# Attention's scores, transposes and products in pairs of PSUM banks, with a re-planned order of the whole kernel

## The chip, the core and the metric

The kernel is one launch on one NeuronCore of a Trainium2 chip. The metric is device time in microseconds (us), from the median of several runs; lower is better. TensorE (PE in the rows) does matmuls, VectorE (DVE) and ScalarE (ACT) do the elementwise work and read PSUM, GpSimd (POOL) helps with elementwise work in SBUF, and SyncE (SP) issues every DMA.

## What is computed

Three stages follow one another: attention, a gated feed-forward (called MoE1 here), and a feed-forward with layer norm and a residual (MoE2). Everything is fp32 on the host side, weights of MoE1 and MoE2 arrive as 64-bit floats.

```python
# attention: q, k, v are [4, 8, 576, 64]
q_d, k_d, v_d = means over groups of 4 positions            # [.., 144, 64]
out_up    = repeat(softmax(q_d k_d^T / 8) v_d, 4)           # coarse part
out_local = softmax(q k^T / 8 where |i - j| < 4) v          # band of 7
x = (out_up + out_local) as [4, 576, 512]
# MoE1
xk, xr = mu * x + (1 - mu) * (x shifted by one position)    # mu_k, mu_r
x1 = sigmoid(xr w_r) * (relu(xk w_k)^2 w_v)                 # w_k, w_v: 512 x 1024, 1024 x 512
# MoE2
out = x1 + relu(layernorm(x1) * g w_ch1) w_ch2              # 512 x 2048, 2048 x 512
```

## The kernel before, in words

**Units of attention.** `attention(n, ...)` (line 453) handles one of 16 units: one batch entry and two heads, which lie on partitions 0 to 63 and 64 to 127. Per unit, in order:

- q and k are loaded and brought to a head-dimension-by-position layout (`qT`, `kT`), by DVE's transpose (line 542) or by TensorE (lines 553 to 562, tile `tq`) depending on the unit's mode `m{n}`. Sums over four positions (`qd`, `kd`) come from DVE or POOL (lines 582 to 585), or, in mode 3, from the same TensorE pass.
- the band: for each head one PSUM bank `sc`. A bf16 matmul with a mask (line 623) opens it, then 24 blocks of 24 queries by 32 keys are added (line 629; the profile counts two matmuls for a block). The contraction runs over 64 partitions, those of the head, and a block writes one of four groups of 32 output partitions. DVE takes the maximum (`mx`, line 640) and subtracts it (`e`, line 643), each once per head; ACT takes the exponential of both heads at once (line 646).
- the coarse part: `ds` (line 655), maximum on DVE (line 667), its scaling on DVE or ACT (lines 668 and 669), three exponentials on ACT (line 673).
- sums and reciprocals on DVE (lines 677 to 681), normalisation, and a transpose of the band into `pT`, copied to `PT`.
- the coarse weights are transposed on TensorE into `tp` in two halves `kt`, one bank each (line 707), each copied to `pdT` by ACT or DVE (lines 711 and 712).
- `up` (line 718) is the coarse product; ACT copies it to `ups`.
- `pv` (line 748) is the band's product in two halves, one bank each; DVE adds `ups` to each half and writes `xT` (line 762). The alternative path `join` is off in all units (`g0` to `g15` are 0).

**MoE1** runs over six chunks of 384 tokens. `prep` (line 785) mixes neighbouring positions on ACT, DVE and POOL. `moe_r` makes `psr`, `moe_k` makes `psk`, `accumulate` (line 847) adds into three banks `psv` (line 778 to 780: each fp32 product is three matmuls of high and low parts), and `moe_x` (line 858) multiplies on DVE and stores. **MoE2** makes `psh` and accumulates `pso` in six banks.

**Weights** come through `load_f32` (line 383): a 512 KB DMA into one of two buffers `w64`, two passes on ACT (lines 395 and 397), two on DVE (402 and 406), then a split into a high and a low part (`load_split`, line 410; low part at line 420). The order of the first loads is by priority, lowest first: `w_r` tile `kt` has `wr + wrs * kt`, the first half of `w_k` has `wka + wkas * kt`.

**PSUM** has 8 banks: three of `ps_v` (`pv0`, `pv1`, `pv2`), two of `ps_k` (`pk`), three of `ps_a` (`pa`). Attention of batch entries 1 to 3 takes its banks from the three of `pa`; batch entry 0 goes round `pa`, `pk`, `pv0` and `pv1` (`psa`, line 444), since MoE1 does not run yet.

**The order of work.** Nothing is issued where it is written. `Plan.add` collects operations with a cost, a priority and the buffers read and written. `Plan.order` (line 123) walks them as a list scheduler: each engine takes the ready operation that can start first, ties by priority, and buffers of one tag are handed out strictly in the order of the priorities of their first users (`turn`). All constants in `PRM` are priorities and choices for this planner. `Plan.issue` (line 228) emits the engines' queues in that order. Each engine then runs its own queue strictly in order. While MoE1's third accumulator is not yet in use, `issue` fills TensorE's planned pauses with dummy matmuls (`warm`, line 433) of 0.14 us planned each; they keep the engine busy and compute nothing. A first batch of 17 is planned at 4.5 us, and in batch entry 0 each `sc` and `ds` group begins with two more.

```python
free = {e: 0.0 for o in ops for e, *_ in o.ways}       # order(): all engines begin at 0
...
for _ in range(int((o.at - free) / fill_cost)):        # issue(): dummy matmuls in a pause
    fill()
```

Of the kernel before, what the change touches and what calls it, by code (L numbers as in the profile page):

```python
# [24 lines left out]
    thin=89.915, t0=-16.294, t1=-9.875, t2=6.158, t3=7.667, t4=48.796, t5=19.99, t6=6.382, t7=-23.592, t8=-0.47,  # L25
    t9=-5.238, t10=-2.702, t11=0.12, t12=5.747, t13=-8.176, t14=-15.681, t15=-4.758, m0=2, m1=1, m2=0, m3=3, m4=1,
    m5=0, m6=0, m7=2, m8=3, m9=0, m10=0, m11=0, m12=0, m13=0, m14=0, m15=0, g0=0, g1=0, g2=0, g3=0, g4=0, g5=0, g6=0,
    g7=0, g8=0, g9=0, g10=0, g11=0, g12=0, g13=0, g14=0, g15=0, h0=1, h1=1, h2=1, h3=1, h4=0, h5=0, h6=0, h7=0, h8=0,
    h9=0, h10=0, h11=0, h12=0, h13=0, h14=0, h15=0, dve=0.27, pool=0, ta=-14.632, u0=4.274, tl=26.492, tm=4222.228,
    ld=33.163, ldv=76.41, mu=-14.605, wr=-0.059, wrs=-31.134, wka=-33.615, wkas=7.94, wkb=12.502, wkbs=-165.286,  # L30
    wv=103.601, wvs=2.875, wld=0.932, d0=235.165, d1=108.349, d2=260.708, d3=463.399, d4=581.694, d5=82886.056,
    a1=13.725, a1s=43.62, a1l=52.7, a2=-1.632, a2s=26.831, a2l=56.61, a3=54.215, a3s=40.382, a3l=96.628, xr=-60.685,
    xrs=16.307, xk=22.171, xks=1.12, xrn=9, xrns=1.512, xkn=-4.695, xkns=17.37, w2a=10.707, w2as=1.55, w2=7.281,
    w2s=34.846, wc=10.079, wcs=106.739, m2q=8, sld=-6.173, x1=3, wcg=-39.001, p0l=11.872, p0=2.352, p0s=3.263,
    p0n=7.723, dp=684.729, ra0=-8.097, ra1=-1.757, ra2=3.642, ra3=4.616, ra4=-5.44, ra5=0, rb0=0.342, rb1=19.209,
    rb2=16.653, rb3=33.463, rb4=10.116, rb5=0, rx0=-2.918, rx1=-13.421, rx2=8.601, rx3=12.062, rx4=-2.926, rx5=5.409,
    ne=12, we=52.842, wes=25.704, wel=6.378,
# [23 lines left out]
class Plan:  # L61
# [8 lines left out]
    SYNC = {"PE": 0.21, "ACT": 0.16, "DVE": 0.14, "POOL": 0.2, "SP": 0.0, "CTL": 0.0}  # L70

# [51 lines left out]
    def order(self):  # L123
# [6 lines left out]
        free = {e: 0.0 for o in ops for e, *_ in o.ways}  # L130
# [10 lines left out]
        for k in sorted(range(nb), key=lambda k: first[k], reverse=True):  # L141
            turn[tag[k]].append(k)
# [85 lines left out]
    def issue(self, fill, fill_cost, until):  # L228

        end, seq = self.order()  # L230
        free = 0.0
        for i in seq:
            o = self.ops[i]
            for b in o.bufs:
                if b.t is None:
                    pool = b.pool if hasattr(b.pool, "tile") else b.pool()
                    b.t = pool.tile(b.shape, b.dtype, name=b.name, tag=b.tag, bufs=b.bufs)
            eng, cost, fn, _ = o.ways[o.way]
            if eng == "PE":
                if until.t is None:  # L240
                    for _ in range(int((o.at - free) / fill_cost)):
                        fill()
                free = o.at + cost
            fn()
        return end
# [20 lines left out]
def attn_moe_kernel(  # L266
# [164 lines left out]
    def warm_up(n=17):  # L431
# [10 lines left out]
    n_ps = [0]  # L442

    def psa(b, name):
        if b > 0:
            return Buf(ps_a, [P, 512], F32, "pa", 3, name)
        ring = [(ps_a, "pa", 3), (ps_k, "pk", 2), (ps_v, "pv0", 1), (ps_a, "pa", 3), (ps_k, "pk", 2),
                (ps_a, "pa", 3), (ps_v, "pv1", 1)]
        pool, tag, n = ring[n_ps[0] % len(ring)]
        n_ps[0] += 1  # L450
        return Buf(pool, [P, 512], F32, tag, n, name)

    def attention(n, T0, TL):
# [19 lines left out]
        join = PRM[f"g{n}"]  # L473

        def load(src, dst):
            if runs:
# [3 lines left out]
                ), w=[dst], lat=2.2)  # L480
                return
            if mode:
                for hp in range(2):
# [3 lines left out]
                    ), w=[(dst, hp)], lat=2.2)  # L487
                return
            for hp in range(2):
                for e in range(2):  # L490
# [4 lines left out]
                    ), w=[(dst, (hp, e))], lat=2.2)  # L495
# [121 lines left out]
        for h in range(2):  # L617
            sc = psa(b, "sc")

            def score(h=h, sc=sc):  # L620
                if first:
                    warm_up(2)
                nc.tensor.matmul(sc()[:, :G * 32], identb, maskb.rearrange("p g c -> p (g c)"),
                                 start=True, stop=False)
                for g in range(G):
                    for j in range(4):
                        i = 4 * g + j
                        m = min(32, S - QB * i)
                        nc.tensor.matmul(
                            sc()[32 * j:32 * j + m, 32 * g:32 * g + 32],  # L630
# [5 lines left out]
            add("PE", 0.8 + hold(2), pr(0.2), score, r=[qT, kT], w=[sc] + held, thin=True)  # L636
            mx = Buf(at, [P, G, 1], F32, "mx", 2)
            scv = lambda sc=sc: sc()[:, :G * 32].rearrange("p (g c) -> p g c", c=32)
            add("DVE", c_dve(192), pr(0.25),
                lambda mx=mx, scv=scv: nc.vector.tensor_reduce(mx()[:, :, 0], scv(), axis=AX.X, op=ALU.max),  # L640
                r=[sc], w=[mx])
            add("DVE", c_dve(192), pr(0.25),
                lambda mx=mx, scv=scv, h=h: nc.vector.tensor_tensor(
                    e()[:, h], scv(), mx().to_broadcast([P, G, 32]), op=ALU.subtract),
                r=[sc, mx], w=[(e, h)])
# [16 lines left out]
        add("PE", 1.0 + hold(2), pr(0.3), dscore, r=[qd, kd], w=[ds_] + held, thin=True)  # L662
# [5 lines left out]
        add([("DVE", 0.2, lambda: nc.vector.tensor_scalar_mul(mxd()[:, 0:3], mxd()[:, 0:3], -0.0078125), False),  # L668
             ("ACT", 0.15, lambda: nc.scalar.mul(mxd()[:, 0:3], mxd()[:, 0:3], -0.0078125), False)],
            0, pr(0.35), None, w=[mxd])  # L670
        for t in range(3):
# [7 lines left out]
        add("DVE", 0.18, pr(0.5), lambda: nc.vector.tensor_scalar_add(stat()[:, 0:15], stat()[:, 0:15], 1e-9),  # L679
            w=[stat])  # L680
# [20 lines left out]
        for kt in range(2):  # L701
            tp = psa(b, "tp")
            tpv = lambda tp=tp: tp()[:HS, :2 * SD].rearrange("p (h c) -> p h c", c=SD)

            def tpose(kt=kt, tpv=tpv):
                for t, q0 in enumerate((0, 64, SD - 64)):
                    nc.tensor.transpose(tpv()[:, :, q0:q0 + 64], pd()[:, t, HS * kt:HS * kt + HS], ident)

            add("PE", 0.47, pr(0.65), tpose, r=[pd], w=[tp], thin=True)

            add([("ACT", c_act(288, True), lambda kt=kt, tpv=tpv: nc.scalar.mul(pdT()[:, kt], tpv(), 0.25), False),
                 ("DVE", c_dve(288), lambda kt=kt, tpv=tpv: nc.vector.tensor_scalar_mul(
                     pdT()[:, kt], tpv(), 0.25), False)], 0, pr(0.7), None, r=[tp], w=[(pdT, kt)])
# [11 lines left out]
        if not join:  # L725
# [8 lines left out]
        for half in range(2):  # L734
            pv = psa(b, "pv")

            def pvmm(half=half, pv=pv):
                for kt in range(2 if join else 0):
                    for hp in range(2):
                        nc.tensor.matmul(  # L740
                            pv()[64 * hp:64 * hp + 64, :288],
                            vd()[:, 2 * hp + kt, :],
                            pdT()[:, kt, hp, 72 * half:72 * half + 72].unsqueeze(2).to_broadcast([HS, 72, 4]),
                            start=(kt == 0), stop=False,
                        )
                for g in range(3 * half, 3 * half + 3):
                    for hp in range(2):
                        nc.tensor.matmul(
                            pv()[64 * hp:64 * hp + 64, 96 * (g % 3):96 * (g % 3) + 96],
                            vw()[:, hp, g, :],  # L750
                            PT[:, hp, g, :],
                            start=not join, stop=not join or g % 3 == 2,
                        )

            if join:
                add("PE", 1.75, pr(0.85), pvmm, r=[vw, PTb, vd, pdT], w=[pv])
                add(psum_copy(288, lambda half=half: x()[:, u, 1 + 288 * half:1 + 288 * half + 288],
                              lambda pv=pv: pv()[:, :288]), 0, pr(0.9), None, r=[pv], w=[(x, (u, half))])
                continue
            add("PE", 0.67, pr(0.85), pvmm, r=[vw, PTb], w=[pv], thin=True)  # L760
            add("DVE", c_dve(288), pr(0.9),
                lambda half=half, pv=pv: nc.vector.tensor_tensor(
                    x()[:, u, 1 + 288 * half:1 + 288 * half + 288].rearrange("p (s r) -> p s r", r=4),
                    pv()[:, :288].rearrange("p (s r) -> p s r", r=4),
                    ups()[:, 72 * half:72 * half + 72].to_broadcast([P, 72, 4]),
                    op=ALU.add), r=[pv, ups], w=[(x, (u, half))])
# [80 lines left out]
    def accumulate(pv, f, last, ab, wt, prio):  # L847
        a, b_ = ab
        wh, wl = wt
        for t in range(TT):  # L850
            add("PE", MW, prio, lambda t=t: mm3(
                pv[t](), a()[:, t * P:t * P + P], b_()[:, t * P:t * P + P], wh(), wl(), f == 0, last),
                r=[a, b_, wh, wl], w=[pv[t]])
# [449 lines left out]
```

## Time and profile before

| | us |
|---|---|
| three runs | 770.59, 773.99, 775.18 (median 773.99) |
| the profiled execution | 771.95 |
| its span, first to last instruction | 770.2 |
| mean granted TensorE clock in it | 0.999 of full speed |

Times in the rows count from the span's start. Times of engines are busy times; a matmul's time in a row covers its way through the array, and matmuls overlap, so the step from one start to the next says what one costs.

### The profile page before, as it was taken

What the parts mean: (1) busy time and instruction counts of PE and PEld (TensorE: products, weight loads), DVE (VectorE), ACT (ScalarE), POOL (GpSimd) and SP (SyncE); (2) the same over time, 40 slices, a digit from 0 to 9 for tenths busy, and PEclk for the clock granted to TensorE, in tenths of its full rate; (3) what the DMA queues carried; (4) which work ended last, traced back from release to release, by engine and by line L of the source; (5) the groups of instructions that cost most, each with busy time, mean ns of one, the idle gap of its engine ahead of it and who ended that gap; (6) DMA issues with size and microseconds to landing.
All of it is one profiled execution on the core that took longest, in us unless ns stands there. A gap on an engine that the chain in (4) does not pass through costs nothing.

```text
span 770.2 us, 15665 instructions
## 1 busy us (share of the span) xinstructions
PE 753.6 (98%) x5816; PEld 650.2 (84%) x5816; DVE 524.6 (68%) x1083; ACT 398.2 (52%) x916; POOL 63.8 (8%) x113
## 2 busy tenths in 40 slices
PE   9999999999999999999999999999999999999997
PEld 6878787788788798888888888889889899889886
DVE  6899999998985959878889763486543364333233
ACT  6889997987884847868835431221421131111110
POOL 3101122112100000000110000020000020000000
PEclk9999999999999999999999999999999999999999
DMA  8997596867768895964689894379853347443322
GB/s 190 208 192 180 180 180 124 182 170 144 207 159 267 251 323 171 290 217 135 141 281 289 208 258 121 112 246 305 183 150 115 112 121 258 138 120 113 123 69 82
DMA packets 202854, 140.88 MB, mean 183 GB/s; under 512 B 127120, under 2 KB 160028, under 8 KB 202780
## 3 DMA queue, kind: packets, MB, share of 16 engines
q1 hardware_dynamic: 202780, 139.90, 66.6%
q8 instruction: 46, 0.75, 0.4%
q14 instruction: 28, 0.23, 0.1%
HBM read 107.88 MB, written 31.98 MB: 182 GB/s over the span
## 4 chain that ended last, share of the span: by engine, by line
PE 77%; DVE 10%; DMA 6%; ACT 4%; issue 2%; POOL 0%; SPq 0%; DVEq 0%; POOLq 0%; ACTq 0%
PE pso L779 8%; PE pso L778 8%; PE pso L780 8%; PE psh L778 7%; PE psh L779 7%; PE psh L780 7%; PE psk L778 4%; PE psv L778 4%; PE psk L780 3%; PE psk L779 3%; PE psv L779 3%; PE psv L780 3%; DMA w<-in_moe_w_ch_dram 3%; PE warm L433 2%; DVE tmu L802 1%
## 5 line engine op out<-in xcount | busy, mean ns | idle before, releaser
L778 PE MATMUL psh<-xn,sa 128*128 128x384 f32 x336 | 114.0, 339 | 2.4 <-DVE c L1114 1.2
L779 PE MATMUL psh<-xn,sa 128*128 128x384 f32 x336 | 113.6, 338 | 0.0
L780 PE MATMUL psh<-xn,sa 128*128 128x384 f32 x336 | 113.3, 337 | 0.0
L778 PEld LDWEIGHTS psh<-xn,sa 128*128 128x128 f32 x336 | 63.1, 188 | 11.0 <-DVE c L1114 2.1
L779 PEld LDWEIGHTS psh<-xn,sa 128*128 128x128 f32 x336 | 63.1, 188 | 6.1 <-DVE xn L1051 0.2
L780 PEld LDWEIGHTS psh<-xn,sa 128*128 128x128 f32 x336 | 63.1, 188 | 0.0
L379 ACT ACTIVATE c22h<-t 128x384 fp32r<-128x384 f32 x24 | 12.6, 525 | 83.7 <-DVE t L1106 78.6
L395 ACT ACTIVATE wf<-w 128x512 f32<-128x512 f32 x48 | 32.3, 673 | 17.4 <-DMA w<-in_moe_w_ch_dram 9.2
L402 DVE SCALAR_TENSOR_TENSOR wf<-wf,w 128x512 uint32<-128x512 uint32 x48 | 32.9, 687 | 11.1 <-ACT w L397 10.6
L379 ACT ACTIVATE kr<-psk 128x384 f32<-128x384 f32 x46 | 22.4, 488 | 25.2 <-PE psk L780 21.2
L379 ACT ACTIVATE c11h<-psh 128x384 fp32r<-128x384 f32 x23 | 11.3, 491 | 45.8 <-PE psh L780 45.7
L397 ACT ACTIVATE w<-w 128x512 uint32<-128x512 uint8 x52 | 35.0, 672 | 0.0
L843 DVE TENSOR_TENSOR kl<-kr,kh 128x384 fp32r<-128x384 f32 x43 | 23.8, 553 | 14.6 <-ACT kr L842 14.3
L1083 DVE SCALAR_TENSOR_TENSOR c11l<-psh,c11h 128x384 fp32r<-128x384 f32 x24 | 13.3, 554 | 29.1 <-ACT c11h L379 29.1
L802 DVE SCALAR_TENSOR_TENSOR tmu<-xT,oms,tmu 128x384 f32<-128x384 f32 (+1 forms) x64 | 31.7, 512 | 1.8 <-ACT tmu L796 1.8
L406 DVE SCALAR_TENSOR_TENSOR wf<-w,wf 128x512 uint32<-128x512 uint32 x48 | 32.7, 680 | 0.3
L1106 DVE TENSOR_TENSOR t<-psh,t 128x384 f32<-128x384 f32 x24 | 13.3, 554 | 28.5 <-PE psh L780 28.4
L1097 DVE TENSOR_TENSOR u<-psh,u 128x384 f32<-128x384 f32 x24 | 13.3, 555 | 27.2 <-PE psh L780 27.1
L379 ACT ACTIVATE c12h<-c 128x384 fp32r<-128x384 f32 x24 | 12.6, 525 | 37.0 <-DVE c L1110 36.9
L379 ACT ACTIVATE c21h<-c 128x384 fp32r<-128x384 f32 x24 | 12.6, 523 | 34.6 <-DVE c L1114 34.6
L796 ACT ACTIVATE tmu<-xT,vecs 128x384 f32<-128x384 f32 (+1 forms) x51 | 26.8, 539 | 6.9 <-DVE xrl L806 4.0
L1103 DVE TENSOR_TENSOR t<-psh,u 128x384 f32<-128x384 f32 x24 | 13.2, 552 | 20.2 <-PE psh L780 20.1
(527 smaller groups left out, 2164.5 us busy)
## 6 DMA issues: line engine op xcount, KB each, us to landing
sa<-s_dram SPq DMA_DIRECT2D x168, 256.0 KB, 2.7
w<-in_moe_w_ch_dram SPq DMA_DIRECT2D x32, 512.0 KB, 6.2
s_dram<-s SPq DMA_DIRECT2D x56, 256.0 KB, 4.0
vw<-in_v_dram SPq DMA_DIRECT2D x62, 96.0 KB, 4.0
x_dram<-r SPq DMA_DIRECT2D x18, 256.0 KB, 3.4
x1t<-x_dram SPq DMA_DIRECT2D x6, 768.0 KB
z_dram<-x1t SPq DMA_DIRECT2D x18, 256.0 KB, 2.7
zb<-z_dram SPq DMA_DIRECT2D x96, 48.0 KB, 2.8
```

The costliest lines, as they stand in the source:

```text
L379: return [("ACT", c_act(n, True), lambda: nc.scalar.activation(dst(), src(), AF.Relu), False), ("DVE", c_dve(n), lambda: nc.vector.tensor_ ...
L395: add("ACT", c_act(512), prio, lambda: nc.scalar.activation(f(), w64().bitcast(F32)[:, :, 1], AF.Abs, scale=2.0 ** -112), r=[w64], w=[f])
L397: add("ACT", c_act(512), prio, lambda: nc.scalar.activation(w64()[:, :, 0], w64().bitcast(U8).rearrange("p a (b c) -> p a b c", c=4)[:, :, ...
L402: lambda: nc.vector.scalar_tensor_tensor(fu(), fu(), 3, w64()[:, :, 0], op0=ALU.logical_shift_left, op1=ALU.bitwise_or),
L406: lambda: nc.vector.scalar_tensor_tensor(fu(), w64()[:, :, 1], 0x80000000, fu(), op0=ALU.bitwise_and, op1=ALU.bitwise_or),
L433: nc.tensor.matmul(warm()[:, :304], identb, isumb, start=True, stop=True)
L778: nc.tensor.matmul(ps, lh, rh, start=start, stop=False, skip_group_check=more)
L779: nc.tensor.matmul(ps, lh, rl, start=False, stop=False, skip_group_check=more)
L780: nc.tensor.matmul(ps, ll, rh, start=False, stop=stop, skip_group_check=more)
L796: add([("ACT", c_act(n, ap=1), lambda t=t, o=o, n=n, cur=cur, kt=kt: nc.scalar.mul(t()[:, o:o + n], cur(), mu[:, kt:kt + 1]), False), ("DV ...
L802: lambda t=t, o=o, n=n, prv=prv, kt=kt: nc.vector.scalar_tensor_tensor(t()[:, o:o + n], prv(), om[:, kt:kt + 1], t()[:, o:o + n], op0=ALU. ...
L843: add(either(C, lambda e: e.tensor_tensor(kl(), kr(), kh().bitcast(F32), op=ALU.subtract)), 0, prio, None, r=[kr, kh], w=[kl])
```

## The change

Attention's `sc`, `tp` and `pv` each take one tile of two neighbouring banks, and one instruction reads both. The scores of the two heads are issued alternately. PSUM is split anew: `ps_a` is one pair `pp` and one single bank `pa`; `ps_v` is one pair `pv` and the single bank `pv2`; MoE1's and MoE2's accumulators become a pair and a single bank. For batch entries 1 to 3 every `tq`, `ds` and `up` uses the single `pa`, and every `sc`, `tp` and `pv` the pair `pp`; batch entry 0 alternates between `pp` and `pv` for the pairs and goes round `pk`, `pk`, `pa` for the rest. Two tiny operations may now run on POOL. The path `join` is dropped. The planner lets each engine begin at a later time of its own, the first batch of dummies is 8, and all constants are new (among them `m1` from 1 to 3, `m4` from 1 to 4).

```diff
-    thin=89.915, ... m1=1, ... m4=1, ... wr=-0.059, wrs=-31.134, wka=-33.615, wkas=7.94, ...
+    thin=44.759, ... m1=3, ... m4=4, ... wr=8.408, wrs=-37.451, wka=39.719, wkas=-29.625, ...
...
+    START = {"PE": 1.78, "ACT": 2.0, "DVE": 2.6, "POOL": 6.6, "SP": 0.74, "CTL": 0.0}
...
-        free = {e: 0.0 for o in ops for e, *_ in o.ways}
+        free = {e: self.START[e] for o in ops for e, *_ in o.ways}
...
-    def warm_up(n=17):
+    def warm_up(n=8):
...
     def psa(b, name):
         if b > 0:
-            return Buf(ps_a, [P, 512], F32, "pa", 3, name)
-        ring = [(ps_a, "pa", 3), (ps_k, "pk", 2), (ps_v, "pv0", 1), (ps_a, "pa", 3), (ps_k, "pk", 2),
-                (ps_a, "pa", 3), (ps_v, "pv1", 1)]
+            return Buf(ps_a, [P, 512], F32, "pa", 1, name)
+        ring = [(ps_k, "pk", 2), (ps_k, "pk", 2), (ps_a, "pa", 1)]
...
+    def psp(b, name):
+        pool, tag = (ps_v, "pv") if b == 0 and n_ps[1] % 2 else (ps_a, "pp")
+        n_ps[1] += 1
+        return Buf(pool, [P, 2, 512], F32, tag, 1, name)
...
-        for h in range(2):
-            sc = psa(b, "sc")
+        sc = psp(b, "sc")
+        def scores():
+            if first:
+                warm_up(2)
+            for h in range(2):
+                nc.tensor.matmul(sc()[:, h, :G * 32], identb, mask, start=True, stop=False)
+            for g in range(G):
+                for j in range(4):
+                    for h in range(2):
+                        nc.tensor.matmul(sc()[32 * j:32 * j + m, h, 32 * g:32 * g + 32],
+                                         qT()[64 * h:64 * h + 64, ...], kT()[64 * h:64 * h + 64, ...],
+                                         start=False, stop=(g == G - 1))
+        add("PE", 1.25 + hold(2), pr(0.2), scores, r=[qT, kT], w=[sc] + held, thin=True)
+        add("DVE", c_dve(384), ...  tensor_reduce(mx()[:, :, :, 0], scv(), max)
+        add("DVE", c_dve(384), ...  tensor_tensor(e(), scv(), mx().to_broadcast([P, 2, G, 32]), subtract)
...
-        add([("DVE", 0.2, ... mxd scale ...), ("ACT", 0.15, ...)], ...)
+        add([("POOL", 0.42, ... mxd scale ...), ("ACT", 0.15, ...)], ...)
-        add("DVE", 0.18, ... stat + 1e-9 ...)
+        add([("DVE", 0.35, ... stat + 1e-9 ...), ("POOL", 0.42, ...)], ...)
...
-        for kt in range(2):
-            tp = psa(b, "tp")        # three transposes, one copy of 288
+        tp = psp(b, "tp")            # six transposes, one copy of 576
...
-        for half in range(2):
-            pv = psa(b, "pv")        # twelve matmuls, one add of 288
+        pv = psp(b, "pv")            # 24 matmuls, one add of 576
...
-        pvs[c] = [Buf(ps_v, [P, 512], F32, f"pv{t}", 1, f"psv{t}") for t in range(TT)]
+        pvs[c] = accs(ps_v, "pv", "pv2", "psv")          # a pair and a single bank
...
-                    pv = [Buf(... f"pv{n}" ... if n < TT else ... "pa", 3 ...) for n in range(2 * TT)]
+                    pv = accs(ps_v, "pv", "pv2", "pso") + accs(ps_a, "pp", "pa", "pso")
-    add("PE", 4.5, -20.0, warm_up, w=[warm])
+    add("PE", 1.55, -20.0, warm_up, w=[warm])
```

## Rows read from the trace of the kernel before

**Rows 1.** The stretches: busy us and instructions by engine, granted clock, DMA share, GB/s.

```profile
0.00:60.00 60.00, 55.79 (x973) 43.35 (x974) 49.16 (x114) 45.03 (x120) 9.57 (x38) 1.00 1.00 196
60.00:235.00 175.00, 171.79 (x2266) 140.57 (x2265) 159.94 (x351) 148.76 (x386) 30.45 (x55) 1.00 0.72 169
235.00:390.00 155.00, 151.62 (x734) 131.90 (x733) 124.64 (x248) 111.41 (x225) 8.85 (x9) 1.00 0.76 227
390.00:771.00 381.00, 374.35 (x1849) 334.37 (x1847) 190.82 (x372) 93.05 (x185) 14.94 (x12) 1.00 0.56 169
```

**Rows 2.** Groups by line on PE: count, busy us, mean ns, idle before them.

```profile
L433 PE MATMUL warm<-isum,identb 128*128 128x304 bf16 x135 | 22.8, 308 | 2.0 <-DVE identb L326 1.8 <-issue 0.2
...
L778 PE MATMUL psk<-xkh,wk00h 128*128 128x384 f32 x24 | 9.2, 381 | 3.2 <-ACT r L822 2.6 <-ACT kr L379 0.6
```

**Rows 3.** The chain that ended last, 45 to 59 us: start us, us, what.

```profile
45.61 6.70 DMA w<-in_moe_w_r_dram
...
52.90 0.26 ACT ups L371
...
55.44 0.37 DVE xT L762
...
57.01 0.84 DVE wr0l L420
```

**Rows 4.** The timeline of PE: the first product of MoE1.

```profile
57.31 0.49 PE L778 MATMUL psr<-wr0h,xrh 128*128 128x512 f32 x1
```

**Rows 5.** The timeline of PE, one unit's scores: start us, us, engine, line, operation.

```profile
105.87 0.26 PE L623 MATMUL sc<-maskb,identb 128*128 128x192 bf16 x1
106.05 0.61 PE L629 MATMUL sc<-kT,qT 64*32 64x32 f32 x48
106.60 0.26 PE L623 MATMUL sc<-maskb,identb 128*128 128x192 bf16 x1
...
107.33 0.46 PE L655 MATMUL ds<-kd,qd 64*64 64x144 f32 x4
```

**Rows 6.** The timeline of PE's weight loads, the same stretch.

```profile
106.05 0.50 PEld L629 LDWEIGHTS sc<-kT,qT 64*32 64x32 f32 x48
```

**Rows 7.** The tile sc: count, duration ns min/median/max, first and last start us.

```profile
L629 PEld LDWEIGHTS sc<-kT,qT x1536: 95/109/110, 10.8 to 219.8; 64*32 64x32 f32 x192
...
L623 PE MATMUL sc<-maskb,identb x32: 243/256/258, 10.6 to 219.2; 128*128 128x192 bf16 x32
```

**Rows 8.** Groups by line on DVE up to 410 us: count, busy us, mean ns.

```profile
L762 DVE TENSOR_TENSOR xT<-pv,ups 128x288 f32<-128x288 f32 x32 | 13.8, 443 | 1.0 <-PE pv L748 0.9
...
L640 DVE TENSOR_REDUCE mx<-sc 128x6 f32<-128x192 f32 x32 | 10.9, 346 | 1.0 <-PE sc L629 0.7
L643 DVE TENSOR_TENSOR e<-sc,mx 128x192 f32<-128x192 f32 x32 | 10.9, 343 | 0.2
...
L684 DVE TENSOR_TENSOR e<-e,stat 128x384 f32<-128x384 f32 x16 | 8.8, 547 | 0.0
L677 DVE TENSOR_REDUCE stat<-e 128x12 f32<-128x384 f32 x16 | 8.6, 537 | 0.2 <-ACT e L646 0.2
...
L585 DVE TENSOR_REDUCE qd<-qT 128x144 f32<-128x576 f32 x10 | 7.4, 740 | 0.0
...
L679 DVE TENSOR_SCALAR stat<-stat 128x15 f32<-128x15 f32 x16 | 4.0, 248 | 0.2 <-ACT pd L673 0.2
```

**Rows 9.** Groups by line on ACT, the same stretch.

```profile
L711 ACT ACTIVATE pdT<-tp 72x288 f32<-72x288 f32 x27 | 10.0, 400 | 1.0 <-PE tp L707 0.8
```

**Rows 10.** The timeline: first write and last read of scores, a later unit.

```profile
168.44 0.26 PE L623 MATMUL sc<-maskb,identb 128*128 128x192 bf16 x1
...
171.52 0.36 DVE L643 TENSOR_TENSOR e<-sc,mx 128x192 f32<-128x192 f32 x1
```

**Rows 11.** The timeline: first write and last read of scores, unit 2.

```profile
25.05 0.25 PE L623 MATMUL sc<-maskb,identb 128*128 128x192 bf16 x1
...
35.53 0.35 DVE L643 TENSOR_TENSOR e<-sc,mx 128x192 f32<-128x192 f32 x1
```

More of the change, by code (lines that the diff above doesn't have):

```diff
@@ L30 @@
[L30 to L34, printed above, removed]
@@ L140, in order @@
         turn = {t: [] for t in slots}
-        for k in sorted(range(nb), key=lambda k: first[k], reverse=True):
+        for k in sorted(range(nb), key=lambda k: (first[k], k), reverse=True):
             turn[tag[k]].append(k)
@@ L634, in score @@
                         )
[L636 to L645, printed above, removed]
+        add("PE", 1.25 + hold(2), pr(0.2), scores, r=[qT, kT], w=[sc] + held, thin=True)
+        mx = Buf(at, [P, 2, G, 1], F32, "mx", 1)
+        scv = lambda: sc()[:, :, :G * 32].rearrange("p h (g c) -> p h g c", c=32)
+        add("DVE", c_dve(384), pr(0.25),
+            lambda: nc.vector.tensor_reduce(mx()[:, :, :, 0], scv(), axis=AX.X, op=ALU.max), r=[sc], w=[mx])
+        add("DVE", c_dve(384), pr(0.25), lambda: nc.vector.tensor_tensor(
+            e(), scv(), mx().to_broadcast([P, 2, G, 32]), op=ALU.subtract), r=[sc, mx], w=[e])
         add("ACT", c_act(384), pr(0.35), lambda: nc.scalar.activation(e(), e(), AF.Exp, scale=0.125), w=[e])
@@ L678, in attention @@
                                             op=ALU.add), r=[e], w=[(stat, 0)])
-        add("DVE", 0.18, pr(0.5), lambda: nc.vector.tensor_scalar_add(stat()[:, 0:15], stat()[:, 0:15], 1e-9),
-            w=[stat])
+        more = lambda e: (lambda: e.tensor_scalar_add(stat()[:, 0:15], stat()[:, 0:15], 1e-9))
+        add([("DVE", 0.35, more(nc.vector), False), ("POOL", 0.42, more(nc.gpsimd), False)], 0, pr(0.5), None, w=[stat])
         add("DVE", 0.2, pr(0.5), lambda: nc.vector.reciprocal(stat()[:, 0:15], stat()[:, 0:15]), w=[stat])
@@ L723, in upper @@
                     )
-        if not join:
+        if True:
             up = psa(b, "up")
@@ L733, in attention @@
         x = xT[b]
-        for half in range(2):
-            pv = psa(b, "pv")
[L737 to L766, printed above, removed]
@@ new lines, in attention, with pvmm @@
+        pv = psp(b, "pv")
+        def pvmm():
+            for g in range(G):
+                for hp in range(2):
+                    nc.tensor.matmul(
+                        pv()[64 * hp:64 * hp + 64, g // 3, 96 * (g % 3):96 * (g % 3) + 96],
+                        vw()[:, hp, g, :], PT[:, hp, g, :], start=True, stop=True)
+        add("PE", 1.4, pr(0.85), pvmm, r=[vw, PTb], w=[pv], thin=True)
+        add("DVE", c_dve(576), pr(0.9),
+            lambda: nc.vector.tensor_tensor(
+                x()[:, u, 1:1 + S].rearrange("p (f s r) -> p f s r", f=2, r=4),
+                pv()[:, :, :288].rearrange("p f (s r) -> p f s r", r=4),
+                ups().rearrange("p (f s) r -> p f s r", f=2).to_broadcast([P, 2, 72, 4]),
+                op=ALU.add), r=[pv, ups], w=[(x, (u, 0)), (x, (u, 1))])
@@ L851, in accumulate, with accs @@
             add("PE", MW, prio, lambda t=t: mm3(
-                pv[t](), a()[:, t * P:t * P + P], b_()[:, t * P:t * P + P], wh(), wl(), f == 0, last),
-                r=[a, b_, wh, wl], w=[pv[t]])
+                pv[t][0](), a()[:, t * P:t * P + P], b_()[:, t * P:t * P + P], wh(), wl(), f == 0, last),
+                r=[a, b_, wh, wl], w=[pv[t][1]])
+    def accs(pool, pair, one, name):
+        b2, b1 = Buf(pool, [P, 2, 512], F32, pair, 1, name), Buf(pool, [P, 512], F32, one, 1, name)
+        return [(lambda: b2()[:, 0], (b2, 0)), (lambda: b2()[:, 1], (b2, 1)), (b1, b1)]
     x1d = Fixed(x1_dram)
```

81 lines of the change are left out of this document (40 added, 41 removed).

## The prediction

> **What bounds the kernel now.** I read the stretches first, then the groups of TensorE by line, then the chain of waits, and last the timelines of single units. The stretches [rows 1] show four stages. From 390 us on, MoE2 keeps PE busy for 374.35 of 381 us, with DVE at half and ACT at a quarter: this stage is matmuls alone, and the change only gives its accumulators other banks. From 235 to 390 us and from 60 to 235 us PE stands idle for no more than 3.4 and 3.2 us, so PE sets the pace there too; but DVE is busy for 159.9 of 175 us in the second of these, ACT for 148.8, and a late elementwise step shows directly as a PE pause (the first `psk` product waits 2.6 us in all on ACT's `r`, and takes 381 ns in the mean [rows 2]). The first 60 us are different: 22.8 us of PE's busy time are dummy matmuls [rows 2]. There PE waits for the start of MoE1, and the chain shows for what: a load of `w_r` that takes 6.7 us and lands at 52.3, ACT's copy of `ups` standing behind it, DVE's add to `xT`, and the low part of `w_r` at 57.0 [rows 3]. Only then begins the work that fills PE (the first `psr` at 57.3 [rows 4]). So a microsecond counts if it is PE work between 60 and 390 us, or if it lies on the chain of the start; a microsecond of PE work among the dummies is worth nothing. All through, the granted clock is full [rows 1].
>
> **Scores.** One head costs 0.73 us from mask to mask (105.87 to 106.60), the two 1.46 (to 107.33, when `ds` begins): 0.18 from a mask to the first score and 0.55 for 48 small matmuls, twice [rows 5]. After the change there are two masks in a row, one change of shape and 96 small matmuls whose row halves alternate. The second mask I put at 0.10, an estimate below the 0.18 that a mask takes together with the change of shape. If the heads' matmuls overlap fully, the 96 take 0.55 and the group 0.83; if they only queue, 1.10 and 1.38. So a unit saves 0.08 to 0.63 us. The nearest row is the issue of the weight loads: 48 of them span 0.50 us [rows 6], one takes 0.109 [rows 7], so one starts every (0.50 - 0.11) / 47 = 8.3 ns. At that rate 96 take 0.80 and a unit saves 0.38. I take 0.35, which is also the middle. Twelve units lie after the start: 12 x 0.35 = 4.2 us, with ends 1.0 and 7.6. The four units of batch entry 0 lie among the dummies: nothing.
>
> The Trainium skill ("TensorE: Matmul & The Clock Gate", Part 3: Packing small matmuls) says that a weight load overlaps matmuls in flight only where the row group differs, and that packed tiles start some 4 ns apart. In the kernel before all 48 scores of a group lie in one row group, and they still come 11 ns apart [rows 5], so the first half of the rule is too strict here; by the second half 96 scores would take 0.38 us, and a unit would save 1.46 - 0.66 = 0.80 us, 9.6 in all, an estimate by that page. The same page (Wait — 56ns, not 53.3ns?) gives a floor of about 25 ns between starts however small the matmul; by it neither form could be as fast as the 11 ns that the rows show, so it is set aside.
>
> **Elementwise work.** Two maxima of 346 ns become one of 384 columns; the sum over 384 columns takes 537 [rows 8]. Two subtractions of 343 become one, as the product over 384 in 547. Saved: 155 + 139 = 294 ns a unit. The two adds of 443 become one of 576 columns: at (537 - 346) / 192 = 1.0 ns a column 443 + 288 = 731, saved 155. Together 0.45 us of DVE a unit, 7.2 us over 16. The addition of 1e-9 (248 ns [rows 8]) may move to POOL, up to 4.0 us more. On ACT two copies of 400 ns [rows 9] become one of at least 400 and at most 800. In unit 1 the sums over four positions (740 ns each [rows 8], on DVE or POOL) give way to TensorE and four short copies.
>
> What reaches the end of it: after the start 12 x 0.45 = 5.4 us of DVE are freed where PE's own idle time is 3.2 + 3.4 us [rows 1]. It can return between nothing and 6.6 us; I take 2, because most of DVE's queue is not what PE waits for. A new order could also lose here: as much again, -4, is the lower end.
>
> **Transposes and products.** Their PE work is the same, in one group instead of two. Where two groups of `tp` stood apart, a change of shape goes, worth up to the 0.18 us of [rows 5]: 12 x 0.1 = 1.2 us, ends 0 and 2.2.
>
> **The start.** Four units free 4 x 0.45 = 1.8 us of DVE, unit 1 up to 1.5 more. The weights come in another order. By the old constants `w_r` tile 0 (-0.06) stands behind all four tiles of `w_k` (-33.6 to -9.8); by the new ones (8.4) only behind two (-49.2 and -19.5), so it is the sixth load instead of the eighth. That is the load on the chain [rows 3]. But unit 3 has its own tail there: `xT` at 55.4, only 1.6 us before the low part. If the load came early and the tail stayed, 1.6 us would be won; if ACT no longer stood waiting for it, up to 6. I take 3, with 0 as the lower end. `w_k` tiles 1 and 0 come behind instead; they are needed after MoE1's first gate products, which cover them. Fewer first dummies (8 instead of 17) cost nothing as long as the fill makes up for them and the granted clock stays full as in [rows 1]; no row shows a unit of attention at a lower clock, and what it would cost would fall among the dummies.
>
> **The accumulators** change banks only. A pair comes free when both its readers are done, but between two uses lie MoE1's gate and first `psk`, or MoE2's first `psh` products, several us long: nothing.
>
> **The sum:** 4.2 + 2 + 1.2 + 3 = 10.4 us, from the profiled execution's 771.95 (span 770.2 and 1.75 around it): 761.6. The median of the runs shown stands 2.0 above that execution; I add half of this for a median of new runs: 762.5.
>
> **Rivals.** *Little happens:* the heads' matmuls queue (1.0 us), the tail of unit 3 holds the start behind another weight load (1 us), and the waits stay: 771.95 - 2 + 1 = 771. For it speaks that PE, DVE and the DMA (share 1.00 in the first 60 us [rows 1]) are all full in the start; against it, that scores surely lose one change of shape.
>
> *The start comes much earlier:* with `w_r` early and ACT not standing behind it, MoE1 begins at 51 instead of 57 (6 us), scores overlap fully (7.6), changes of shape go (2.2) and waits fall by 4: 771.95 - 19.8 + 1 = 753. For it: the chain [rows 3] has a DMA and ACT's wait in it. Against: all ends at once.
>
> *The pair becomes the bound (slower):* three groups of each unit share one pair that is handed out strictly in the planner's order. A unit starts every (219.2 - 10.6) / 15 = 13.9 us (the last row of [rows 7] has the first and last mask). Scores hold their banks for 3.4 us where DVE comes quickly [rows 10], but for 10.8 us in unit 2 (25.05 to 35.88 [rows 11]). The mechanism decides from a mean hold of 13.9 / 3 = 4.6 us. Its price: in the start one hold of 10.8 instead of 3.4 in front of the next unit's groups, 7.4 us on the chain; afterwards each late unit delays a `prep`, and PE has no dummies any more; 12 units at 0.8 us are 9.6. With 4.2 + 1.2 saved as above: 771.95 + 7.4 + 9.6 - 5.4 + 1 = 784.5; at half the price it is 776. For it: three banks shrink to one pair and one bank. Against: the pair's readers are fewer and shorter, and attention is not on the chain between its batch entries.
>
> **How the numbers follow.** The forecast 0.50 (own range 756 to 769), little 0.22, much earlier 0.12, the pair as bound 0.16. A measurement of this kernel tells about 1% (7.7 us) from no change, so faster ends at 766.3. Of the forecast's 0.50 some 0.42 lie below that; with the early start 0.54. Slower by over 1% is above 781.7: the pair's case at over four fifths of its price, or with a lost order (-4) beside it, 0.13. The rest, 0.33, lies within 1%. The range leaves out the far half of the early start and the far part of the pair's case: 752 to 783.
>
> **What would show it.** Scores: one group of masks and 96 matmuls of 1.0 to 1.2 us; 0.83 would say full overlap, 1.38 none. DVE: one maximum and one subtraction of about 540 ns, an add of about 730, and DVE's total 7 to 11 us lower. The start: the first `psr` at about 54 instead of 57.3, and fewer than 20 us of dummies. MoE2: unchanged at some 380 us. The prediction is wrong if the first `psr` is later than 58, if PE has idle stretches before `sc`, `tp` or `pv` released by DVE's read of the pair, or if pauses between 60 and 390 us grow by more than 4 us.

## The result: slower by 1.2%, and the profile after

The changed kernel takes 779.24 us (median of 6 runs, 778.38 to 787.03) beside 771.27 us (770.19 to 775.18) for the kernel before on the same chip: ratio 1.0121, 95% interval 1.0092 to 1.0149. Its profiled execution is 778.71 us (span 776.9), 6.8 us above that of before.

The stretches after, which answer to [rows 1], with one more of 20 us:

```profile
0.00:60.00 60.00, 57.04 (x896) 45.16 (x897) 47.36 (x97) 41.51 (x111) 11.26 (x41) 1.00 0.92 185
60.00:235.00 175.00, 165.77 (x2336) 134.88 (x2335) 158.94 (x306) 147.99 (x373) 33.71 (x68) 0.99 0.76 177
235.00:390.00 155.00, 152.44 (x740) 133.18 (x739) 120.06 (x243) 111.10 (x223) 5.49 (x5) 1.00 0.72 214
...
80.00:100.00 20.00, 15.48 (x184) 11.64 (x187) 19.39 (x37) 17.10 (x42) 3.43 (x5) 0.91 0.62 161
```

TensorE's idle time between 60 and 235 us grew from 3.2 to 9.2 us, two thirds of the growth between 80 and 100 us (4.5 us idle; 0.6 before). There the granted clock fell too: to 0.5, the lower of its two levels, from 88.3 to 91.7 us. TensorE had stood still for 1.9 us (2.3 without a weight load) and was standing still again, for 1.0 us. I counted TensorE's instructions of both kernels at the step that each kind usually has in the kernel after. By that count, an estimate good to about 1 us, the two are level at 80 us; after is 4.3 us behind at 100, 5.2 at 250 and 4.2 at 760; the last 10 us add 1.9. So the loss has two places, and the pauses of both show in TensorE's waits and timeline.

TensorE's waits from 60 to 400 us in the kernel after (who, for whom: us in total, times, longest):

```profile
PE up L727 <- ACT pdT L720: 2.2, 3, 1.9
PE pv L748 <- ACT w L399: 1.6, 1, 1.6
PE psk L770 <- ACT kr L381: 1.3, 2, 0.8
PE tp L716 <- DVE xT L754: 1.3, 2, 1.1
PE tp L716 <- ACT pd L700: 1.0, 1, 1.0
...
PE psv L770 <- DVE r L858: 0.7, 1, 0.7
PE pv L748 <- ACT pdT L720: 0.7, 1, 0.7
```

The timeline of after in three places: one unit's scores, the pair handed from one unit to the next, and the last accumulation round:

```profile
83.47 0.81 PE L716 MATMUL tp<-isum,pd 128*72 128x128 f32 x6
...
86.15 0.64 ACT L720 ACTIVATE pdT<-tp 72x576 f32<-72x576 f32 x1
...
86.84 0.71 PE L727 MATMUL up<-pdT,vd 72*64 72x144 f32 x8 [1.85 <-ACT pdT L720]
...
91.60 1.24 PE L748 MATMUL pv<-PT,vw 128*64 128x96 f32 x24
95.58 0.76 DVE L754 TENSOR_TENSOR xT<-pv,ups 128x576 f32<-128x576 f32 x1
...
96.55 1.21 PE L748 MATMUL pv<-PT,vw 128*64 128x96 f32 x24 [1.62 <-ACT w L399]
...
110.73 0.34 PE L633 MATMUL sc<-maskb,identb 128*128 128x192 bf16 x2
...
111.00 1.01 PE L641 MATMUL sc<-kT,qT 64*32 64x32 f32 x96
...
111.94 0.95 PE L664 MATMUL ds<-kd,qd 64*64 64x144 f32 x12
...
764.55 0.39 PE L772 MATMUL pso<-w27h,c12l 128*128 128x512 f32 x1
764.98 0.69 DVE L1135 TENSOR_TENSOR res<-pso,res 128x512 f32<-128x512 f32 x1 [1.75 <-PE pso L772]
...
765.72 0.50 PE L770 MATMUL pso<-w215h,c22h 128*128 128x512 f32 x1 [0.79 <-DVE res L1135]
```

- `tp` of unit 4 is done at 84.3, but its one copy stands behind other work in ACT's queue until 86.15, and `up` with it.
- `pv` of unit 5 starts 0.21 us after VectorE's read of the pair that unit 4's `pv` left (96.34). The label names ACT's `w`, which ended last; the pair's release is what fits, and e2 below shows it. The wait of 1.1 us before `tp`, on VectorE's `xT`, is for the pair as well. Over the 36 uses of the pair after 60 us (first write to end of last read, from the timeline) `sc` holds it 3.96 us in the mean, `tp` 2.32, `pv` 3.86.
- The scores take 1.21 us (110.73 to 111.94) where [rows 5] had 1.46.
- At 765.72 and again at 770.93 (0.78) a product into the second half of an accumulator pair waits until VectorE has read the first half. With the restarts that costs 1.9 us, and there is nothing behind it to absorb it. The halves are two banks: the Trainium skill ("PSUM — Partial Sum Buffer", Terms) keeps two engines apart within a bank and quadrant, and would ask for no wait here. The wait comes with the tile, which the program follows as one.

VectorE and the dummies after, up to 410 us, which answer to [rows 2, 8, 9]:

```profile
L435 PE MATMUL warm<-isum,identb 128*128 128x304 bf16 x145 | 25.4, 315 | 1.8 <-DVE identb L328 1.8
...
L754 DVE TENSOR_TENSOR xT<-pv,ups 128x576 f32<-128x576 f32 x16 | 12.0, 753 | 0.5 <-PE pv L748 0.3
...
L720 ACT ACTIVATE pdT<-tp 72x576 f32<-72x576 f32 x16 | 10.3, 642 | 1.0 <-PE tp L716 0.9
...
L652 DVE TENSOR_REDUCE mx<-sc 128x12 f32<-128x384 f32 x16 | 8.8, 550 | 1.0 <-PE sc L641 0.8
L653 DVE TENSOR_TENSOR e<-sc,mx 128x384 f32<-128x384 f32 x16 | 8.7, 543 | 0.1
```

And the start. A chunk of MoE1 has three gate tiles `psr`. The first begins at 49.90 (57.31 in [rows 4]) and the second at 51.38, but both need the last quarter of `xr`, which comes from unit 3's `xT`. That tail stayed: the products on this quarter (those with `wr3`) and the third tile begin when they did before. The timeline of after, and that of before:

```profile
56.22 0.76 DVE L754 TENSOR_TENSOR xT<-pv,ups 128x576 f32<-128x576 f32 x1
...
60.45 0.50 PE L770 MATMUL psr<-wr3h,xrh 128*128 128x512 f32 x1
...
63.22 0.50 PE L770 MATMUL psr<-wr0h,xrh 128*128 128x512 f32 x1 [0.58 <-ACT r L814]
```

```profile
60.53 0.39 PE L778 MATMUL psr<-wr3h,xrh 128*128 128x512 f32 x1
...
63.25 0.39 PE L778 MATMUL psr<-wr0h,xrh 128*128 128x512 f32 x1
```

The chain after shows what the third tile waits for:

```profile
48.89 6.86 DMA w<-in_moe_w_k_dram
...
55.77 0.67 ACT wf L397
56.43 0.40 ACT wk10h L377
56.83 5.14 DMA w<-in_moe_w_v_dram
...
61.99 0.68 ACT wf L397
62.68 0.49 ACT r L814
...
63.22 0.50 PE psr L770
```

ACT stands in its queue behind two weight loads, and `r`, which frees the bank for the third tile, stands behind that work. The dummies grew instead of shrinking.

### The profile page after: what moved, and what is told of

The parts are those of the page before. It is cut to its first block, busy times and chain, and to the rows that moved or that the text cites. A ratio compares the mean times of both kernels' runs of the same rounds, so it can differ in the third digit from the quotient of the medians.

```text
span 776.9 us, 15598 instructions
## 1 busy us (share of the span) xinstructions
PE 755.9 (97%) x5838; PEld 651.4 (84%) x5838; DVE 521.2 (67%) x1025; ACT 395.0 (51%) x894; POOL 67.1 (9%) x128
## 4 chain that ended last, share of the span: by engine, by line
PE 83%; DVE 10%; ACT 4%; DMA 2%; issue 1%; POOL 0%; SPq 0%; DVEq 0%; POOLq 0%; ACTq 0%
PE pso L770 9%; PE pso L771 8%; PE pso L772 8%; PE psh L771 7%; PE psh L770 7%; PE psh L772 7%; PE psk L770 4%; PE psk L772 4%; PE psk L771 4%; PE psv L770 4%; PE psv L772 3%; PE psv L771 3%; PE warm L435 2%; PE sc L641 2%; PE ds L664 1%
## 5 line engine op out<-in xcount | busy, mean ns | idle before, releaser
L408 DVE SCALAR_TENSOR_TENSOR wf<-w,wf 128x512 uint32<-128x512 uint32 x48 | 34.4, 717 | 0.4
L435 PE MATMUL warm<-isum,identb 128*128 128x304 bf16 x145 | 25.4, 315 | 1.8 <-DVE identb L328 1.8
## 6 DMA issues: line engine op xcount, KB each, us to landing
x1t<-x_dram SPq DMA_DIRECT2D x6, 768.0 KB, 4.6
```

The source lines that it names most:

```text
L408: lambda: nc.vector.scalar_tensor_tensor(fu(), w64()[:, :, 1], 0x80000000, fu(), op0=ALU.bitwise_and, op1=ALU.bitwise_or),
L435: nc.tensor.matmul(warm()[:, :304], identb, isumb, start=True, stop=True)
```

## The experiments

Two ways of editing recur. Where a kernel has "its order written out", the planner's list of operations (which, on which engine, how many dummies ahead) stands in the kernel and no planning takes place. "Re-ordered" means that such a list was moved about, one operation at a time past its neighbours, and a move kept where the kernel's own planning model ended earlier; the model was given the durations of the traces and the later beginnings. It gives 763.4 us for the order of before and 768.0 for that of after. Its numbers are the planner's, not the chip's.

**One cost or wait at a time, in the planned order of the kernel after.**

```diff
 e1: each add of the last round reads the whole pair
-            r=[pv[n][1]], w=[key])
+            r=[pv[n][1][0] if p == NP - 1 and n % TT < 2 else pv[n][1]], w=[key])
 e2: in upper, tpose, pvmm, ahead of the first product
+            if n == 4: busy(15, up()[:, :304])
+            if n == 5: busy(6, tp()[:, 0, :304])
+            if n == 5: busy(10, pv()[:, 0, :304])
 e3: scores head after head
-            for g in range(G): for j in range(4): for h in range(2): ...
+            for h in range(2): for g in range(G): for j in range(4): ...
 e6: in scores, units 4 to 15
+                busy(4, sc()[:, 0, :304])
 e7: no maximum; zeros are added
-            nc.vector.tensor_reduce(mx()[:, :, :, 0], scv(), axis=AX.X, op=ALU.max)
-            e(), scv(), mx().to_broadcast([P, 2, G, 32]), op=ALU.subtract
+            e(), scv(), zeros, op=ALU.add
```

> In the last accumulation round each add of the output reads the whole pair of banks, so it stands behind the products of both halves; nothing else differs, and the order on TensorE is that of the changed kernel. If the new waits at the end (0.79 and 0.78 us before pso, with the step around each 0.94) lie on the path that sets the end, as the accumulator theory says, the two waits are gone and the time is 1.6 to 1.9 us below the changed kernel's, ratio to the kernel before about 1.010. If the adds behind them set the end anyway, as the rival says, the time stays within 0.5 us of the changed kernel's.

Measured 780.78 us, ratio 1.0134 (1.0112 to 1.0156). In the trace TensorE has no pause after 750 us any more, so the 1.9 us at the end are gone; but this execution was 3.4 us later than the other at 760 us (1.4 at the last product), and the total shows no gain. The cost of the waits is shown by the trace; that removing them shortens the total is not, within some 2 us.

> The changed kernel with 15, 6 and 10 dummy products put in front of the upper products of unit 4, the transposes and the window products of unit 5, into banks that these overwrite, in the order as it is: the pauses of 2.3, 1.0 and 1.6 us between 84 and 97 us stay, but TensorE works in them. If the pauses let the clock fall (theory), the granted clock stays at 1.00 from 84 to 98 us, where it was 0.57 in two stretches of 2 us, and the work standing at 100 us is 1.5 to 2 us further on; the time falls by 1 to 2 us, to a ratio of about 1.010. If the clock falls for another reason (rival), the 0.57 stays, and the time is the changed kernel's or up to 0.5 us more.

Measured 782.10 us, ratio 1.0149 (1.0129 to 1.0169). The stretch of 80 to 100 us, which in after had 15.48 and 0.91:

```profile
80.00:100.00 20.00, 17.48 (x152) 12.83 (x150) 18.03 (x34) 15.99 (x39) 3.51 (x5) 1.00 0.62 158
```

The clock stays full when TensorE works through the first two pauses, so these are what let it fall. TensorE's products have the same order in both kernels, so the same product can be compared: in e2 it stands 0.1 us later than in after at 80 us and 0.2 us earlier at 94. The two filled pauses and the full clock together are thus worth 0.3 us: the fallen clock was a companion of the loss and not its cause. The third batch did not fill its pause. It writes into the pair and waits for it:

```profile
96.52 1.47 PE L439 MATMUL pv<-isum,identb 128*128 128x304 bf16 x10 [1.83 <-DVE xT L764]
```

So unit 5's `pv` waits in after for the pair, which VectorE's `xT` still reads. In e2 it comes 1.4 us later for the dummies, and the kernel is still 1.3 us behind at 180 us. The total contains this, so it can't say what the clock is worth.

> The changed kernel with its scores head after head into the same pair, and the same planned order. If alternating the heads is what shortened the scores, a unit's scores take 1.45 to 1.5 us again in place of 1.2 and the time rises by 0.28 x 12 = 3.4 us (units 4 to 15; the first four lie in the start) to at most 4.5 us, ratio about 1.0165. If what was saved on TensorE had turned into pauses (rival), part of it is covered by them, and the time rises by under 1.5 us.

Measured 782.46 us, ratio 1.0150 (1.0118 to 1.0181). The same unit's scores in the timeline:

```profile
111.27 0.34 PE L633 MATMUL sc<-maskb,identb 128*128 128x192 bf16 x2
...
111.54 1.01 PE L641 MATMUL sc<-kT,qT 64*32 64x32 f32 x96
...
112.48 0.71 PE L664 MATMUL ds<-kd,qd 64*64 64x144 f32 x8
```

1.21 us (111.27 to 112.48), as with alternating heads. Both expectations fall: alternating saves nothing. What saves 0.25 us a unit is that both masks stand in front and the 96 matmuls run in one piece: 0.27 + 0.94 instead of twice 0.18 + 0.55. The Trainium skill's rule on row groups ("TensorE: Matmul & The Clock Gate", Part 3: Packing small matmuls), on which alternating would pay, finds no support here.

> The changed kernel with four dummy products of 304 columns (0.127 us each) ahead of the scores of units 4 to 15, into the bank that these overwrite, in the planned order as it is: 12 x 0.51 = 6.1 us more on TensorE between 60 and 235 us, twice what the change saved there. If TensorE sets the pace, the time rises by 5 to 6 us, ratio about 1.020. If DVE and ScalarE set it, at least half of it goes into pauses that are there anyway and the time rises by 0 to 3 us.

Measured 784.24 us, ratio 1.0177 (1.0151 to 1.0203), 0.0056 or 4.3 us above the changed kernel's ratio. Between the two expectations: a microsecond of TensorE's work in this stretch counts for some two thirds, with wide bounds. In the traces the same product is 0.8 us behind that of after at 66 us and 5.6 at 235. The dummies write into the scores' pair and so hold it longer too; how much of the loss is due to that is not shown.

> The changed kernel without the maximum over the scores (left out; a zero is added in place of the subtraction), in the planned order as it is: VectorE has 0.55 us less in each unit, 12 x 0.55 = 6.6 us between 60 and 235 us and 2.2 us before, and TensorE exactly the same. If VectorE sets the pace of that stretch, the time falls by 4 to 7 us, ratio about 1.005. If TensorE sets it, the time falls by under 1.5 us, to a ratio of at least 1.010.

Measured 778.80 us, ratio 1.0107 (1.0080 to 1.0133): 1.1 us less, not told from nothing. VectorE alone does not set the pace, and the pause before `up` stayed at 1.9 us.

**One part of the change alone, on the kernel before.**

```diff
 e4, e5: the order of before written out; for all units (e4) or units 4 to 13 (e5)
-        for h in range(2): sc = psa(b, "sc"); add("PE", 0.8 + hold(2), ..., score, w=[sc] + held)
+        scs = [psa(b, "sc") for h in range(2)]
+        add("PE", ..., scores, w=scs + held)      # both masks, then 96 matmuls
 e10: PRM of before in the kernel after
 e11: START, free = self.START[...] in the kernel before
```

> The kernel before in its own order, written out, with one edit: a unit's two score groups are one group with the heads alternating, into the same two single banks, in the place of the second. No pairs, no new constants, no new beginnings. Theory (the pairs' gain is real and the new plan lost it): 0.28 us a unit saved on a TensorE that has few pauses, 3 to 4.5 us faster than the kernel before, ratio 0.995. Rival (TensorE's time in the attention stretch is no bound, other engines are): within 1 us of the kernel before, and the pauses of the stretch from 60 to 390 us grow by what the scores save.

Measured 773.50 us, ratio 1.0033 (1.0017 to 1.0049): slower. The scores take 1.21 us, but unit 2's two groups had stood 7 us apart, and joining them made the start 3.4 us later; in the last two units the group waits up to 0.8 us for its second bank. So e5 leaves these units out.

> The kernel before in its own order, written out, with one edit: the two score groups of units 4 to 13 are one group (both masks, then the heads alternating) into the same two single banks, in the place of the second group. The first four units and the last two, where the one-group version waited for a second bank or stood in the start, are as before. TensorE has 10 x 0.25 = 2.5 us less to do between 60 and 200 us. If TensorE's work sets the pace there (the prediction's premise), the time is 2 to 3 us below the kernel before, ratio 0.9970. If another engine does (DVE is busy 19 of 20 us there), the 2.5 us turn into pauses and the ratio is 0.999 to 1.001.

Measured 770.20 us beside 769.51, ratio 1.0008 (0.9992 to 1.0024). 2.5 us less work for TensorE in its own order, and nothing gained: the ratio is the second expectation's. But the pauses did not grow: TensorE is idle for 3.2 us between 60 and 235 us, as before. In the two traces, one execution each, the same product stands 1.5 us later in e5 at 94 us, though nothing in the start was changed, and 0.8 us earlier at 220. So what took up the 2.5 us is not shown.

> The changed kernel with the planning constants of the kernel before: pairs, new beginnings and costs stay, only the numbers from which the order is planned are put back. The kernel's own plan then ends at 775.8 in place of 768.0 us. If the plan's end says what the chip does, 7 to 9 us slower than the changed kernel, ratio about 1.022. If the new constants are the loss, as the first theory would have it, it is not slower than the changed kernel, ratio up to 1.012.

Measured 790.58 us, ratio 1.0253 (1.0218 to 1.0288). So pairs with the old constants are worse still: the new constants were needed.

> The kernel before with the later beginnings of the engines alone (constants, banks and costs as before). Its plan ends at 768.3 in place of 767.6 us. If the beginnings were worth the 3 us that the prediction put on the start, ratio about 0.996; if they only shift the order a little, within 1.5 us, ratio 0.998 to 1.002.

Measured 772.24 us, ratio 1.0018 (0.9997 to 1.0039): no change that can be told.

**Order against banks.** e8, e12: the kernel after (with e1's edit), re-ordered; e12's model also knows that a product into one half of an accumulator pair waits for a read of the other. e13: as e12, with MoE1's accumulators in three single banks; batch entry 0 then has one pair in place of two, and goes round five single buffers in place of three. e9, e14: the kernel before, re-ordered, e14 further than e9. e15: e14 with e4's scores in units 4 to 15. The edit of each is the list of operations, in place of `PRM` and `order`:

```diff
-        end, seq = self.order()
-        for i in seq:
+        for i, way, n in ORDER:      # written out: operation, engine, dummies ahead
```

> The changed kernel's own instructions (with the adds of the last round reading whole pairs, as in e1), in another order: the operations of the first 390 us were moved one at a time past their neighbours on the same engine wherever the kernel's planning model, fed with the durations of the traces, came out earlier. That model gives 768.0 us for the changed kernel's order and 752.2 for this one, with TensorE's planned pauses from 60 to 235 us down from 12 to 5 us. If the order that was planned is what lost the gain (theory), the time falls by 8 to 14 us, ratio 0.995 to 1.002, and the pauses before up, tp and pv between 80 and 100 us (4.5 us) are under 1.5 us. If the pairs themselves lose it, by being held (rival: one pair and one single bank where three single banks were), the waits come back elsewhere and the time stays within 3 us of the changed kernel's.

Measured 779.36 us, ratio 1.0110 (1.0077 to 1.0142): the time that the rival expects. TensorE's waits from 60 to 400 us:

```profile
PE psv L875 <- DVE r L963: 5.5, 3, 2.6
PE up L832 <- ACT pdT L825: 3.0, 3, 1.3
PE pv L853 <- ACT w L504: 1.4, 1, 1.4
```

> The kernel before, its own instructions and single banks, with the same treatment of its order: the model gives 763.4 us for the order it has and 750.8 for this one. If pairs are worth their 4 us of TensorE's time once both are ordered equally well, this is 2 to 5 us slower than e8. If sharing one pair costs what the scores save, it is as fast as e8 or up to 3 us faster. Against the kernel before, the theory that order is what counts expects 6 to 11 us, ratio 0.986 to 0.992; the rival that the model is too coarse for that expects within 3 us.

Measured 766.95 us, ratio 0.9957 (0.9933 to 0.9981). Against the kernel before that is 3.3 us, less than the theory expects. Against e8 it is 12.4 us for the same treatment, outside both expectations: more than a better order separates the two kernels. The first wait of e8 is the accumulator pair at the change of MoE1's chunks, which the planner doesn't know: it books the halves apart, and the tile doesn't.

> As e8, but the planning model now holds that a product into one half of an accumulator pair waits for VectorE's read of the other half (in e8's trace TensorE waited 5.5 us before psv for that read, three times); it gives 750.9 us, as for single banks (750.2). If the shared accumulators were what kept e8 at 779 us, this comes to the kernel with single banks of e9, 765 to 769 us, ratio 0.993 to 1.000, with under 1 us of waits before psv. If the attention's own pairs cost more than the model sees, the waits before up, pv and ds stay and the time is 773 us or more, ratio above 1.004.

Measured 771.99 us beside 772.05, ratio 1.0001 (0.9981 to 1.0021). Its waits from 60 to 400 us:

```profile
PE pv L854 <- DMA qin<-in_q_dram: 1.5, 1, 1.5
PE tp L822 <- ACT pd L806: 1.3, 3, 0.7
PE psv L876 <- DVE r L964: 0.8, 1, 0.8
PE tq L671 <- ACT pd L788: 0.7, 1, 0.7
PE ds L770 <- DVE qd L701: 0.7, 1, 0.7
PE up L833 <- ACT pdT L826: 0.5, 1, 0.5
```

The result lies between the two expectations. The waits before `psv` went from 5.5 to 0.8 us, and the ratio by 0.0109, some 8 us; the order differs elsewhere too, so not all of the 8 us is shown to be this wait. With it in the plan the pairs lose nothing against before. They don't win either, though TensorE has 3 us less to do for the scores.

> Attention in one pair and one single bank as in the changed kernel, but the accumulators of the first MoE in three single banks, as before the change (in the second MoE the last three accumulators are still the attention's pair and bank, read whole in the last round); the order moved about as in e12 (model 755.2 us). If the accumulators are the larger part of the loss, no wait before psv on VectorE's read is left and the time is 767 to 773 us; if the attention's pairs are, it is as slow as e12 or slower, 774 us or more.

Measured 777.83 us, ratio 1.0079 (1.0052 to 1.0105). No wait before `psv` is left, yet it is slower than e12. But its order is 4.3 us worse by the model, and with one pair in the start its first `psr` comes at 54.67 us, 6.6 later than e12's (48.11). It doesn't tell accumulators from attention; that split stays open.

> The kernel before, single banks, its order moved further in the same way than in e9 (model 750.2 in place of 750.8 us). A second order of the same quality: within 3 us of e9's 767 us if such an order's gain can be repeated, ratio 0.992 to 0.999; back at 770 us or more if e9 was luck.

Measured 766.18 us beside 772.05, ratio 0.9928 (0.9913 to 0.9944): faster than both kernels, and e9 was no luck.

> Single banks as in e14, with the scores of units 4 to 15 as one group over two single banks (e4's edit, 12 x 0.25 = 3 us less on TensorE) and the order moved for that (model 750.8 us). If TensorE sets the pace once its pauses are gone, 2 to 3 us below e14; if holding two banks at once costs what it saves, within 1.5 us of e14 or slower.

Measured 765.95 us, ratio 0.9931 (0.9907 to 0.9956), as e14. Again 3 us less for TensorE bring nothing that can be told; by the two intervals a gain of 2 us is not excluded.

TensorE's idle time between 60 and 110 us, from the stretches: 5.1 us in the kernel after, 4.1, 4.3 and 4.8 in e8, e12 and e13; with single banks 0.6 before, 0.8, 0.3 and 0.9 in e9, e14 and e15. One exception: pairs with the old constants (e10) have 1.5. So pairs do not force these pauses, but every order made for them that came near the kernel before has them.

## Why the prediction was wrong

- **"A microsecond counts if it is PE work between 60 and 390 us."** This step failed first. e5 took 2.5 us out and won nothing, e15 took out 3 us with no gain that can be told, e6 put 6.1 in and lost about 4. In that stretch ACT and VectorE are nearly as full as TensorE, which is the likely reason; it is not shown, since in e5 TensorE's pauses did not grow. The scores saved 0.25 us a unit where I took 0.35, so 3.0 us and not 4.2, and these did not reach the end.
- **Scores, the reason.** I expected the alternating row halves to shorten them; e3 shows that the alternation makes no difference. That the amount came near was luck: it was worked out from the rate of weight loads, and what saved was one piece in place of two.
- **"What reaches the end of it … I take 2."** Each duration came as worked out (550, 543 and 753 ns where I had some 540, 547 and 731; ACT's copy 642, inside 400 to 800). The three together fell by 6.1 us (35.6 in [rows 8], 29.5 after). But VectorE's total fell by 3.4 us (524.6 to 521.2), not 7 to 11, since other work on it grew under the new plan, and the waits grew by 6.0 us (3.2 to 9.2) instead of falling by 2, more than my lower end of 4. I had freed time and not asked what one larger copy, and one pair, make the next step wait for.
- **Transposes** gave nothing. I counted twelve units, but in the kernel before nine of them had both groups in a row already, 0.58 us from start to start (109.70 to 110.28); the six of one group now take 0.57 (83.47 to 84.04). Where they stood apart (81.88 and 82.90), each group took 0.24.
- **The start.** The first gate product came 7.4 us earlier, where I had 3 and a rival 6, but a first product is not a start: the products on unit 3's quarter came at 60.45 (60.53 before), the third tile at 63.22 (63.25), and at 80 us the kernels were about level. I had named unit 3's tail and counted 1.6 us if it stayed; it stayed and left nothing of that. I had followed the chain to the load of `w_r` and not past it to that tail and to the loads that then stand ahead of ACT.
- **"The accumulators change banks only … nothing."** Wrong, and the clearest error: I looked at how long a pair is free between two uses, and not at a product into one half against a read of the other. It costs 1.9 us at the end and 0.7 before `psv`, and 5.5 us of waits in an order that doesn't know of it (e8; 0.8 in e12).
- **The rival of the pair** was the nearest: 776 at half its price, 784.5 at the full. My threshold, a mean hold of 4.6 us, supposed units evenly spaced. From 136 to 231 us the pair is used 24 times, held for 79.0 of 95.3 us, 3.3 us at a time, and 22 of the 23 times that it is handed on, the next group starts within 1.5 us of its release. That it sets the pace there is not shown: by the count above only 0.9 us is lost between 100 and 250 us, and no run takes the pair away alone. What its release does end is 2.9 us of TensorE's waits (1.6 before `pv`, 1.3 before `tp`). That was one of my signs of being wrong, and so was the growth of the pauses from 60 to 390 us, 5.2 us (6.6 to 11.8).

What decides is thus the planned order with the waits that the pairs add: e12 gets the 1.2% back with pairs, by its order and e1's edit; e14 gets 0.7% more with single banks, in an order that the model puts within 1 us of e12's (750.2 and 750.9). Of the change's 1.2%, how much belongs to the accumulators and how much to the attention's pair was not separated.

## What to carry to other kernels

Before counting freed time on the busiest engine as won, take a little of it out alone, or put some in: where three engines are 85 to 98% busy, it need not reach the end. When two buffers become halves of one tile, list every write to one half that can meet a read of the other, and tell the planner. Compare two layouts only after each has an order made for it. Follow a chain past its first load: what stands just behind it may hold the time that you hope to win.

## What was not expected of the hardware

Small score matmuls run at the same pace whether their row halves alternate or not (1.21 us for 98 in both). The granted clock fell to its lower level at the second of two pauses of 1.9 and 1.0 us on TensorE and stayed full when dummies filled them, and that brought TensorE only 0.3 us forward (e2).
